# The opening of a two-branch kernel at the grain of one row: row 0 of 128 tokens ahead of row 1

## The chip, the cores and the metric

The kernel runs on one core of a Trainium2 chip. The metric is device time in microseconds (us) for one execution; the median of three runs of the kernel before is 198.41 us (198.15 to 198.58). Engines are named as in the profile: PE (matrix multiplication), PEld (its weight loads), DVE (vector engine), ACT (scalar engine, activation functions and copies), POOL, and SP, whose queue issues most loads.

## The reference, cut to what matters

```python
def reference(A_q, A_k, A_v, A_shift_k, A_ssm_k, A_ssm_D, B_x, B_w1, B_b1, B_w2, B_b2):
    ...
    x = A_q                                   # [1, 2048, 640] bf16
    xn = _layernorm(x, axis=-1)
    s = _A_ref(xn, A_k, A_v, A_shift_k, A_ssm_k, A_ssm_D)
    g = _silu(_B_ref(xn, B_w1, B_b1, B_w2, B_b2))
    return x + s * g
```

`_A_ref` multiplies a four-tap shifted k with v, convolves the product along the 2048 tokens with a 2048-long filter per channel (the reference does it by FFT), adds a D term and gates the result with xn. `_B_ref` is a feed-forward block, 640 to 1728 to 640, with a gelu between. Both branches read the normalised x, so the kernel opens with the normalisation.

## The kernel before, in words

The 2048 tokens lie as 16 tokens to each of 128 partitions. A "row" here is one token of each partition, a tile of 128 tokens by 640 channels; a "chunk" is four rows. The kernel computes the convolution as a two-stage transform by matmuls with sine and cosine matrices, and the feed-forward block chunk by chunk. After a function `prologue`, a hand-written order, `PLAN`, lists some 1,200 steps; each step issues its instructions, and each engine runs its own in that order. `PLAN` is not touched here. Each engine takes its instructions strictly in the order in which the program issues them for it, so an instruction that waits holds up all that stand behind it on the same engine.

`prologue` (L740 to L862) handles chunk 0 and prepares constants. What the change and the prediction's steps touch:

- `load_x` (L236) loads a chunk of x on SP's queue. Chunk 0 comes in two loads, rows 0 and 1, then rows 2 and 3. Behind them on the same queue stand three pieces of w1 (L266: columns 0 to 384, 384 to 768, the rest), then chunk 1, k and others.
- `build_f1_product` (L301) makes, after two index rows from POOL, a table of 16 x 128 products in one DVE instruction (L304). Its result is masked later (`f1_phase`, L308) and becomes the argument of sines on ACT at 28 us.
- `bn`, `ag` (L748, L751): statistics of half a row on DVE, two to a row, and their merge. `sq` (L754) takes the square root of variance plus epsilon on ACT, `rc` (L757) its reciprocal on DVE; both handle two rows at once. `norm_dve` (L760) normalises a row in place on DVE.
- `warm` (L766) issues matmuls of 512 columns whose result nobody reads; `WARM = (6, 7)` gives their numbers ahead of and behind the turning of the tap weights (L811).
- `turn` (L774) transposes one row into five 128 x 128 tiles on PE. Tiles 0 to 2 of two rows lie side by side in bank 6 of PSUM, tiles 3 and 4 in bank 7. `turned_out` (L780) copies one bank for both rows to xnT, bank 6 on DVE (L148) and bank 7 on ACT (L147).
- `first_block(x, i)` (L783) multiplies two rows (256 columns) with the i-th 128 columns of w1, five matmuls into bank i. Blocks 0 to 4 of rows 0 and 1 run ahead of the turning of rows 2 and 3, block 5 behind it, and then all six for rows 2 and 3.
- `tap` (L644) spreads tap weights over the partitions by four matmuls into banks 2 to 5; `tap_out` (L763) copies banks 2 and 3, then 4 and 5, to SBUF on ACT.
- `small_bits`, `small_first`, `small_second` (L347, L358, L365) are tiny DVE instructions that prepare the index tables of the small transform matrices. The first instruction of `small_second` is L356.
- An ACT instruction without a use (L848) brings the gelu table in ahead of the first gelu (L479). `pt` (L814) is the place in bank 7 where the biases are turned (L851), and L854 and L855 copy them out.

Behind `prologue`, DVE goes on with `s` (L377 to L385), `f1_phase` (L308), the statistics of chunk 1 (L421), its first products of k and the taps (L594), and the normalisation of rows 4 and 6 (L444), for which PE waits with the transposes of chunk 1 (L451).

Of the kernel before, what the change touches and what calls it, by code (L numbers as in the profile page):

```python
# [26 lines left out]
SIN_EPS = 2.0 ** -20  # L27

NSLOT = 48
WARM = (6, 7)  # L30
NFIRST = 6

TURNS = "231221331312001123202202330111320201303303312100"
# [58 lines left out]
def kernel(  # L92
# [15 lines left out]
    nc = tc.nc  # L108

    CH = 4  # L110
# [34 lines left out]
    def evac(eng, out_ap, in_ap):  # L145
        if eng == "a":
            return nc.scalar.copy(out=out_ap, in_=in_ap)  # L147
        return nc.vector.tensor_copy(out=out_ap, in_=in_ap)  # L148
# [3 lines left out]
    banks = psum.tile([P, 8, 512], F32, name="banks")  # L152
# [7 lines left out]
    ident = consts.tile([P, P], BF16, name="ident")  # L160
# [73 lines left out]
        return one(key).bitcast(BF16)  # L234

    def load_x(c):  # L236
        for h in range(1 if c else 2):
            js = slice(2 * h, CH if c else 2 * h + 2)
            nc.sync.dma_start(out=xn_tiles[c][:, js, :], in_=x_v[:, c * CH:(c + 1) * CH, :][:, js, :])

    def load_k(i):
# [56 lines left out]
    s16 = scratch([NJ], F32)  # L298
    r2 = scratch([P], F32)

    def build_f1_product():  # L301
        nc.gpsimd.iota(s16, pattern=[[1, NJ]], base=0, channel_multiplier=NJ, allow_small_or_imprecise_dtypes=True)
        nc.gpsimd.iota(r2, pattern=[[2, P]], base=1, channel_multiplier=0, allow_small_or_imprecise_dtypes=True)
        nc.vector.tensor_tensor(out=prod, in0=s16[:, :, None].to_broadcast([P, NJ, P]),  # L304
                                in1=r2[:, None, :].to_broadcast([P, NJ, P]), op=ALU.mult)
# [41 lines left out]
    def small_bits(*masks):  # L347
        for mask in masks:
            i = scratch([1], I32)
            nc.vector.tensor_single_scalar(out=i, in_=sm["kcol"], scalar=mask, op=ALU.bitwise_and)  # L350
# [7 lines left out]
    def small_first():  # L358
        n_in, c_in, r_in = sm["in"]
        n_out, c_out, r_out = sm["cols"]  # L360
        sm.update(ph=scratch([3, P], F32), mask=scratch([3, P], F32), c8=scratch([1], F32), c16=scratch([1], F32))
        nc.vector.tensor_single_scalar(out=sm["c8"], in_=c_in, scalar=8.0, op=ALU.mult)
        nc.vector.tensor_single_scalar(out=sm["c16"], in_=c_in, scalar=16.0, op=ALU.mult)
# [280 lines left out]
    def tap(j, h, ps):  # L644
        nc.tensor.matmul(out=ps[:, 0:HALF], lhsT=ident[0:4, j:j + 1].to_broadcast([4, P]), rhs=skT[:, half(h)],
                         start=True, stop=True)
# [93 lines left out]
    def prologue():  # L740
# [6 lines left out]
        def bn(j, h):  # L747
            nc.vector.bn_stats(out=stats[:, j, h, :], in_=xn[:, j, h * HALF:(h + 1) * HALF])  # L748

        def ag(j):  # L750
            nc.vector.bn_aggr(out=mv[:, j, :], in_=stats[:, j, :, :])  # L751

        def sq(a):
            nc.scalar.activation(out=sd[:, a:a + 2], in_=mv[:, a:a + 2, 1], func=ACT.Sqrt, bias=eps[:])  # L754

        def rc(a):
            nc.vector.reciprocal(out=rstd[:, a:a + 2], in_=sd[:, a:a + 2])  # L757

        def norm_dve(j):
            nc.vector.tensor_scalar(out=xn[:, j, :], in0=xn[:, j, :], scalar1=mv[:, j, 0:1],  # L760
                                    scalar2=rstd[:, j:j + 1], op0=ALU.subtract, op1=ALU.mult)

        def tap_out(j):  # L763
            nc.scalar.copy(out=halves(w_exp[:, j, :]), in_=banks[:, 2 * j + 2:2 * j + 4, 0:HALF])

        def warm(n, bank=7):  # L766
            for _ in range(n):
                nc.tensor.matmul(out=banks[:, bank, :].rearrange("p (a b) -> p a b", a=4), lhsT=ident[:],
                                 rhs=ident[:, None, :].to_broadcast([P, 4, P]), start=True, stop=True)

        split = (0, 3, DT)
        tp = [banks[:, 6 + b, :].bitcast(BF16).rearrange("p (t c) -> p t c", t=4) for b in range(2)]

        def turn(q):  # L774
            for t in range(DT):
                b = int(t >= split[1])
                nc.tensor.transpose(out=tp[b][:, t - split[b], q % 2 * P:(q % 2 + 1) * P],
                                    in_=xn[:, q, t * P:(t + 1) * P], identity=ident[:])

        def turned_out(eng, b, x):  # L780
            evac(eng, xnT[:, split[b]:split[b + 1], x * 2 * P:(x + 1) * 2 * P], tp[b][:, 0:split[b + 1] - split[b], :])

        def first_block(x, i):  # L783
            cols = slice(x * 2 * P, (x + 1) * 2 * P)
            for t in range(DT):
                nc.tensor.matmul(out=banks[:, i, cols], lhsT=w1_sb[:, t, i * P:(i + 1) * P], rhs=xnT[:, t, cols],
                                 start=(t == 0), stop=(t == DT - 1))
# [60 lines left out]
        nc.scalar.activation(out=sd[:, 0:1], in_=eps[:], func=ACT.Gelu_apprx_tanh)  # L848
        turn(2)
        turn(3)  # L850
        nc.tensor.transpose(out=pt[:, 0:FT + DT], in_=prm[:, :], identity=ident[0:FT + DT, 0:FT + DT])  # L851
        turned_out("d", 0, 1)
        turned_out("a", 1, 1)
        nc.vector.tensor_copy(out=b1_f[:], in_=pt[:, 0:FT])  # L854
# [56 lines left out]
```

## Time and profile before

| | |
|---|---|
| median of 3 runs | 198.41 us (198.15 to 198.58) |
| the profiled execution's own time | 198.26 us |
| its span in the profile | 196.5 us |
| granted clock of PE over the span | 0.998 |
| busy: PE, DVE, ACT, POOL | 186.5, 175.3, 162.6, 42.9 us |

A row of an engine's answer in order of time gives start, length, engine, line, operation, operands and how many instructions stand together; in brackets is the idle time ahead of the first and what ended it. Instructions of an engine overlap a little, so that several together take less than their single times. A row of busy time by stretch gives the stretch, its length, then the busy time of PE, PEld, DVE, ACT and POOL with the number of instructions, the granted PE clock, the share of DMA time and GB/s. A row of a group gives line, engine, operation, operands and shapes, the number, then busy us and mean ns of one, then the idle time ahead of them and its enders. A row of a load gives the median time from issue to landing at its end. In the chain of waits a row gives start, length and what ran.

### The profile page before, as it was taken

What the parts mean: (1) busy time and instruction counts of PE and PEld (TensorE: products, weight loads), DVE (VectorE), ACT (ScalarE), POOL (GpSimd) and SP (SyncE); (2) the same over time, 40 slices, a digit from 0 to 9 for tenths busy, and PEclk for the clock granted to TensorE, in tenths of its full rate; (3) what the DMA queues carried; (4) which work ended last, traced back from release to release, by engine and by line L of the source; (5) the groups of instructions that cost most, each with busy time, mean ns of one, the idle gap of its engine ahead of it and who ended that gap; (6) DMA issues with size and microseconds to landing.
All of it is one profiled execution on the core that took longest, in us unless ns stands there. A gap on an engine that the chain in (4) does not pass through costs nothing.

```text
span 196.5 us, 5128 instructions
## 1 busy us (share of the span) xinstructions
PE 186.5 (95%) x1927; PEld 111.1 (57%) x1939; DVE 175.3 (89%) x379; ACT 162.6 (83%) x323; POOL 42.9 (22%) x76
## 2 busy tenths in 40 slices
PE   7899969999999999998999999999999999999991
PEld 2585447787665445663566443465665544657771
DVE  7989999999999999989999999999999920489992
ACT  3577999999999999999998999999679758991030
POOL 8100300004454032344030000000475500002220
PEclk9999999999999999999999999999999999999999
DMA  6999999974888899798788999596969659994344
GB/s 200 374 378 345 342 408 414 393 294 153 319 326 337 268 325 368 303 341 341 267 274 312 287 338 329 158 303 228 272 243 336 223 188 350 397 398 157 145 173 137
DMA packets 27057, 57.69 MB, mean 294 GB/s; under 512 B 3032, under 2 KB 15513, under 8 KB 27032
## 3 DMA queue, kind: packets, MB, share of 16 engines
q1 hardware_dynamic: 22528, 39.65, 57.6%
q0 software_dynamic: 4320, 17.70, 24.3%
q8 instruction: 15, 0.25, 0.5%
q14 instruction: 10, 0.08, 0.2%
q10 hardware_dynamic: 184, 0.01, 0.1%
HBM read 33.76 MB, written 18.35 MB: 265 GB/s over the span
## 4 chain that ended last, share of the span: by engine, by line
PE 59%; ACT 14%; DMA 12%; DVE 9%; issue 3%; SPq 1%; DVEq 0%
PE banks L500 20%; PE banks L467 19%; ACT area L147 7%; PE banks L414 7%; DMA area<-in_A_k_dram 5%; DMA area<-in_A_ssm_k_dram 5%; PE banks L550 5%; DVE area L590 3%; DMA w_sb<-in_B_w_dram 2%; ACT hT L479 2%; DVE area L594 2%; PE banks L719 2%; PE banks L720 2%; DVE area L148 2%; PE banks L451 1%
## 5 line engine op out<-in xcount | busy, mean ns | idle before, releaser
L147 ACT CAST area<-banks 128x426 bf16<-128x426 f32 (+2 forms) x175 | 80.7, 614 | 4.2 <-PE banks L414 3.4
L500 PE MATMUL banks<-w_sb,hT 128*128 128x320 bf16 (+1 forms) x462 | 65.8, 295 | 0.4 <-ACT sl L508 0.3
L500 PEld LDWEIGHTS <-hT 128*128 128x128 bf16 x462 | 43.5, 98 | 18.9 <-issue 3.7
L467 PE MATMUL banks<-xnT,w_sb 128*128 128x512 bf16 x218 | 52.8, 379 | 0.7
L674 DVE TENSOR_TENSOR area<-banks,area 128x426 bf16<-128x426 f32 (+1 forms) x96 | 50.1, 591 | 0.2
L479 ACT ACTIVATE hT<-banks,b_f 128x512 bf16<-128x512 f32 x52 | 35.4, 718 | 4.9 <-PE banks L467 3.0
L467 PEld LDWEIGHTS <-w_sb 128*128 128x128 bf16 x230 | 21.5, 97 | 25.7 <-issue 3.7
L508 ACT ACTIVATE sl<-banks 128x320 bf16<-128x320 f32 (+1 forms) x33 | 14.8, 476 | 14.2 <-PE banks L500 12.9
L594 DVE TENSOR_TENSOR area<-area 128x1280 bf16<-128x1280 bf16 x32 | 25.4, 816 | 0.3
L414 PE MATMUL banks<-area,mats 32*32 32x426 bf16 (+1 forms) x768 | 20.7, 345 | 0.5 <-DVE area L148 0.2
L728 DVE TENSOR_TENSOR area<-banks,xn 128x426 bf16<-128x426 f32 (+1 forms) x18 | 9.9, 591 | 12.3 <-ACT hT L479 10.2
L704 POOL DMA_DIRECT2D scrC<-area x16 | 11.7, 730 | 42.1 <-ACT area L147 40.0
L590 DVE TENSOR_TENSOR area<-area 128x1280 bf16<-128x1280 bf16 x24 | 19.1, 812 | 0.0
L550 PE MATMUL banks<-area,WA 128*128 128x212 bf16 (+1 forms) x64 | 15.6, 299 | 0.1
L550 PE MATMUL banks<-area,WB 128*128 128x214 bf16 (+1 forms) x64 | 15.5, 299 | 0.0
L565 POOL DMA_DIRECT2D scrK<-area x16 | 8.8, 553 | 29.3 <-ACT area L147 28.9
L414 PEld LDWEIGHTS <-mats 32*32 32x32 bf16 x768 | 8.1, 88 | 12.4 <-issue 10.3
L148 DVE CAST area<-banks 128x426 bf16<-128x426 f32 (+1 forms) x21 | 11.4, 593 | 1.6 <-PE banks L414 0.8
L576 POOL DMA_DIRECT2D scrU<-area x16 | 8.6, 543 | 14.5 <-ACT area L147 13.7
L430 POOL TENSOR_TENSOR rs<-ve,mhalf 128x4 f32<-128x4 f32 x3 | 4.0, 1350 | 31.0 <-DVE ve L426 31.0
L421 DVE BATCH_NORM_STATS2 st<-xn 128x6 f32<-128x320 bf16 x24 | 10.3, 472 | 0.0
L515 DVE TENSOR_TENSOR xn<-xn,sl 128x320 bf16<-128x320 bf16 (+1 forms) x33 | 9.8, 307 | 0.2 <-ACT sl L508 0.2
(106 smaller groups left out, 195.8 us busy)
## 6 DMA issues: line engine op xcount, KB each, us to landing
scrK<-area POOLq DMA_DIRECT2D x16, 320.0 KB, 3.2
scrU<-area POOLq DMA_DIRECT2D x16, 320.0 KB, 3.7
area<-scrK SPq DMA_DIRECT2D x16, 320.0 KB, 6.6
area<-area SPq DMA_DIRECT2D x32, 160.0 KB, 3.8
area<-scrU SPq DMA_DIRECT2D x16, 320.0 KB, 4.8
scrC<-area POOLq DMA_DIRECT2D x16, 320.0 KB, 4.2
area<-scrC SPq DMA_DIRECT2D x16, 320.0 KB, 6.5
area<-in_A_k_dram SPq DMA_DIRECT2D x4, 640.0 KB, 10.0
```

Source lines behind the costliest of these rows:

```text
L147: return nc.scalar.copy(out=out_ap, in_=in_ap)
L148: return nc.vector.tensor_copy(out=out_ap, in_=in_ap)
L414: nc.tensor.matmul(out=out[b, :], lhsT=mats[a, m, a], rhs=rhs[a, :], start=start, stop=stop)
L467: nc.tensor.matmul(out=ps, lhsT=w1_sb[:, t, ft * P:(ft + 1) * P], rhs=xnT[:, t, :], start=(t == 0), stop=(t == DT - 1))
L479: nc.scalar.activation(out=hT[:, ft, :], in_=one(("h", i)), func=ACT.Gelu_apprx_tanh, bias=b1_f[:, ft:ft + 1], scale=1.0)
L500: nc.tensor.matmul(out=ps[:, 0:ws.stop - ws.start], lhsT=hT[0:M, ft, q * P:(q + 1) * P], rhs=w2_sb[0:M, ft, hs.start + ws.start:hs.start + ...
L508: nc.scalar.activation(out=sl[:, ws], in_=one(key)[:, 0:ws.stop - ws.start], func=ACT.Silu)
L550: nc.tensor.matmul(out=ps[:, dst], lhsT=(WA, WB)[r][:, n2, :], rhs=rows[:, n2 % 2, src], start=True, stop=True)
L590: nc.vector.tensor_tensor(out=uc, in0=uc, in1=tmp, op=ALU.add)
L594: nc.vector.tensor_tensor(out=tmp if s else uc, in0=kh[:, r0:r0 + KC, :], in1=w_exp[:, j:j + 1, :].to_broadcast([P, KC, D]), op=ALU.mult)
L674: nc.vector.tensor_tensor(out=flat(("p", i))[:, x * w:x * w + w], in0=one(("mu", i))[:, 0:w], in1=flat(key)[:, cols(j)], op=ALU.mult)
L704: nc.gpsimd.dma_start(out=pair_view(scrC)[g2], in_=pair(("c", g2)))
```

## The change

Chunk 0 is loaded as row 0 alone and rows 1 to 3 together. Square root and reciprocal are taken for row 0, for row 1, and for rows 2 and 3 together. A row's five transposed tiles now lie in one bank, bank 6 for even rows and bank 7 for odd ones; `turned_out` copies a range of tiles of one row: rows 0 and 1 in two pieces each on ACT, rows 2 and 3 in one piece each on DVE. `first_block` takes a range of rows: blocks 0 to 3 run for row 0 and for row 1 apart (128 columns), blocks 4 and 5 for both together. The product table is made in two instructions, 12 of its 16 parts at the old place and 4 behind the copies of rows 2 and 3, with `small_first` behind it. The warm-up matmuls are 6, 3 and 1 in place of 6 and 7. In DVE's order row 1's first statistics stand ahead of row 0's reciprocal, and row 2's first statistics ahead of row 1's. In ACT's order row 1's square root stands ahead of the copies of row 0, and the square root of rows 2 and 3 ahead of the second tap copy.

```diff
-WARM = (6, 7)
+WARM = (6, 3, 1)
...
     def load_x(c):
-        for h in range(1 if c else 2):
-            js = slice(2 * h, CH if c else 2 * h + 2)
+        for js in ((slice(0, CH),) if c else (slice(0, 1), slice(1, CH))):
             nc.sync.dma_start(out=xn_tiles[c][:, js, :], in_=x_v[:, c * CH:(c + 1) * CH, :][:, js, :])
...
-    def build_f1_product():
+    SPLIT = 12
+
+    def f1_indices():
...
+    def f1_product(a, b):
+        nc.vector.tensor_tensor(out=prod[:, a:b, :], in0=s16[:, a:b, None].to_broadcast([P, b - a, P]),
+                                in1=r2[:, None, :].to_broadcast([P, b - a, P]), op=ALU.mult)
...
-        def sq(a):
-            nc.scalar.activation(out=sd[:, a:a + 2], in_=mv[:, a:a + 2, 1], func=ACT.Sqrt, bias=eps[:])
+        def sq(a, n):
+            nc.scalar.activation(out=sd[:, a:a + n], in_=mv[:, a:a + n, 1], func=ACT.Sqrt, bias=eps[:])
...
-        tp = [banks[:, 6 + b, :].bitcast(BF16).rearrange("p (t c) -> p t c", t=4) for b in range(2)]
+        tp = [banks[:, 6 + b, :].bitcast(BF16)[:, 0:D].rearrange("p (t c) -> p t c", t=DT) for b in range(2)]
...
-        def turned_out(eng, b, x):
-            evac(eng, xnT[:, split[b]:split[b + 1], x * 2 * P:(x + 1) * 2 * P], tp[b][:, 0:split[b + 1] - split[b], :])
-
-        def first_block(x, i):
-            cols = slice(x * 2 * P, (x + 1) * 2 * P)
+        def turned_out(eng, q, a, b):
+            evac(eng, xnT[:, a:b, q * P:(q + 1) * P], tp[q % 2][:, a:b, :])
+
+        def first_block(i, lo, hi):
+            cols = slice(lo * P, hi * P)
...
-        build_f1_product()
+        f1_indices()
+        f1_product(0, SPLIT)
...
+        bn(0, 0)
+        bn(0, 1)
+        ag(0)
+        sq(0, 1)
         warm(WARM[0])
...
         warm(WARM[1])
-        pt = banks[:, 7, :].bitcast(BF16)[:, 4 * P:]
-        for j in (0, 1):
-            bn(j, 0)
-            bn(j, 1)
-            ag(j)
-        small_bits(30)
-        sq(0)
-        rc(0)
+        pt = banks[:, 7, :].bitcast(BF16)[:, D:]
+        bn(1, 0)
+        rc(0, 1)
         norm_dve(0)
-        norm_dve(1)
+        bn(1, 1)
+        ag(1)
+        sq(1, 1)
         turn(0)
-        turn(1)
...
+        warm(WARM[2])
         bn(2, 0)
-        turned_out("d", 0, 0)
-        turned_out("a", 1, 0)
+        turned_out("a", 0, 0, 3)
+        turned_out("a", 0, 3, DT)
         tap_out(0)
-        tap_out(1)
+        rc(1, 1)
+        norm_dve(1)
         bn(2, 1)
         ag(2)
         bn(3, 0)
+        first_block(0, 0, 1)
+        turn(1)
+        first_block(1, 0, 1)
+        turned_out("a", 1, 0, 3)
+        turned_out("a", 1, 3, DT)
         bn(3, 1)
         ag(3)
-        small_bits(1)
-        for i in range(NFIRST - 1):
-            first_block(0, i)
-        sq(2)
-        rc(2)
+        small_bits(30, 1)
+        sq(2, 2)
+        for i in (2, 3):
+            first_block(i, 0, 1)
+        tap_out(1)
+        for i in range(4):
+            first_block(i, 1, 2)
+        rc(2, 2)
         norm_dve(2)
         norm_dve(3)
         small_bits(96)
-        small_first()
-        nc.scalar.activation(out=sd[:, 0:1], in_=eps[:], func=ACT.Gelu_apprx_tanh)
+        first_block(4, 0, 2)
         turn(2)
         turn(3)
...
-        turned_out("d", 0, 1)
-        turned_out("a", 1, 1)
+        turned_out("d", 2, 0, DT)
+        turned_out("d", 3, 0, DT)
+        nc.scalar.activation(out=sd[:, 0:1], in_=eps[:], func=ACT.Gelu_apprx_tanh)
...
-        first_block(0, NFIRST - 1)
+        first_block(5, 0, 2)
+        f1_product(SPLIT, NJ)
+        small_first()
         small_second()
         for i in range(NFIRST):
-            first_block(1, i)
+            first_block(i, 2, CH)
```

More of the change, by code (lines that the diff above doesn't have):

```diff
@@ L751, in ag, with rc @@
             nc.vector.bn_aggr(out=mv[:, j, :], in_=stats[:, j, :, :])
-        def sq(a):
-            nc.scalar.activation(out=sd[:, a:a + 2], in_=mv[:, a:a + 2, 1], func=ACT.Sqrt, bias=eps[:])
-        def rc(a):
-            nc.vector.reciprocal(out=rstd[:, a:a + 2], in_=sd[:, a:a + 2])
+        def sq(a, n):
+            nc.scalar.activation(out=sd[:, a:a + n], in_=mv[:, a:a + n, 1], func=ACT.Sqrt, bias=eps[:])
+        def rc(a, n):
+            nc.vector.reciprocal(out=rstd[:, a:a + n], in_=sd[:, a:a + n])
         def norm_dve(j):
@@ L769, in warm @@
                                  rhs=ident[:, None, :].to_broadcast([P, 4, P]), start=True, stop=True)
-        split = (0, 3, DT)
-        tp = [banks[:, 6 + b, :].bitcast(BF16).rearrange("p (t c) -> p t c", t=4) for b in range(2)]
+        tp = [banks[:, 6 + b, :].bitcast(BF16)[:, 0:D].rearrange("p (t c) -> p t c", t=DT) for b in range(2)]
         def turn(q):
             for t in range(DT):
-                b = int(t >= split[1])
-                nc.tensor.transpose(out=tp[b][:, t - split[b], q % 2 * P:(q % 2 + 1) * P],
-                                    in_=xn[:, q, t * P:(t + 1) * P], identity=ident[:])
-        def turned_out(eng, b, x):
-            evac(eng, xnT[:, split[b]:split[b + 1], x * 2 * P:(x + 1) * 2 * P], tp[b][:, 0:split[b + 1] - split[b], :])
-        def first_block(x, i):
-            cols = slice(x * 2 * P, (x + 1) * 2 * P)
+                nc.tensor.transpose(out=tp[q % 2][:, t, :], in_=xn[:, q, t * P:(t + 1) * P], identity=ident[:])
+        def turned_out(eng, q, a, b):
+            evac(eng, xnT[:, a:b, q * P:(q + 1) * P], tp[q % 2][:, a:b, :])
+        def first_block(i, lo, hi):
+            cols = slice(lo * P, hi * P)
             for t in range(DT):
```

2 lines of the change are left out of this document (removed).

## The prediction

> **What bounds the kernel now.** I read the busy time by stretch first, then the order of time engine by engine over the first 27 us, then the waits.
>
> ```profile
> PE 186.5 (95%) x1927; PEld 111.1 (57%) x1939; DVE 175.3 (89%) x379; ACT 162.6 (83%) x323; POOL 42.9 (22%) x76
> ...
> 40.00:60.00 20.00, 19.87 (x153) 13.93 (x153) 19.93 (x37) 20.00 (x51) 8.27 (x15) 1.00 0.70 270
> ...
> 160.00:180.00 20.00, 19.82 (x129) 11.64 (x128) 9.45 (x18) 15.90 (x27) 0.58 (x2) 1.00 0.84 312
> ```
>
> From 40 us on, the matmul engine (first of the busy times behind the length) is busy for 99% of each stretch shown. Nothing after the opening is edited, so what the change is worth is how much sooner or later that full stretch begins. Its beginning is here:
>
> ```profile
> 26.52 1.31 PE L451 MATMUL banks<-ident,xn 128*128 128x128 bf16 x16 [1.45 <-DVE xn L444]
> ...
> 12.71 0.17 DVE L854 CAST b_f<-banks 128x14 f32<-128x14 bf16 x1 [0.29 <-ACT xnT L147]
> ...
> 12.87 0.60 DVE L356 SCALAR_TENSOR_TENSOR area<-area 128x128 f32<-128x128 f32 x2
> 16.56 0.88 DVE L421 BATCH_NORM_STATS2 st<-xn 128x6 f32<-128x320 bf16 x2
> 26.02 0.80 DVE L444 TENSOR_SCALAR xn<-xn,mv,rs 128x640 bf16<-128x640 bf16 x2
> ```
>
> The matmul engine runs dry at 25.07 and stands still for 1.45 us until DVE has normalised the second chunk (L444). DVE's answer shows no idle mark between 12.71 and 26.02, so DVE is a full line from L854 to L444. **The kernel's start-up is therefore DVE's line**, and the number to find is the moment at which DVE begins L356 (`small_second`), now 12.87. A lead of the matmul engine alone only lengthens its own 1.45 us of waiting.
>
> **What leads up to 12.87 now.**
>
> ```profile
> 1.64 2.29 DVE L304 TENSOR_TENSOR area<-area 128x2048 int32<-128x2048 f32 x1 [0.64 <-POOL area L303]
> 3.85 0.88 DVE L748 BATCH_NORM_STATS2 stats<-xn 128x6 f32<-128x320 bf16 x2
> 4.77 0.21 DVE L751 BATCH_NORM_AGGREGATE mv<-stats 128x2 f32<-128x12 f32 x1
> 4.89 0.83 DVE L748 BATCH_NORM_STATS2 stats<-xn 128x6 f32<-128x320 bf16 x2
> 6.39 0.17 DVE L757 RECIPROCAL rstd<-sd 128x2 f32<-128x2 f32 x1 [0.21 <-ACT sd L754]
> 6.60 0.80 DVE L760 TENSOR_SCALAR xn<-xn,mv,rstd 128x640 bf16<-128x640 bf16 x2
> ...
> 11.56 0.14 DVE L362 TENSOR_SCALAR area<-area 128x1 f32<-128x1 f32 x1
> 11.87 0.56 DVE L148 COPY xnT<-banks 128x768 bf16<-128x768 bf16 x1
> ...
> 1.35 2.74 PE L768 MATMUL banks<-ident 128*128 128x512 bf16 x6 [1.35 <-POOL ident masks.py:199]
> 4.65 1.69 PE L768 MATMUL banks<-ident 128*128 128x512 bf16 x7
> 7.10 0.81 PE L777 MATMUL banks<-ident,xn 128*128 128x128 bf16 x10 [0.77 <-DVE xn L760]
> 7.84 0.71 PE L645 MATMUL banks<-skT,ident 4*128 4x320 bf16 x4
> 8.48 2.90 PE L786 MATMUL banks<-xnT,w_sb 128*128 128x256 bf16 x25
> 11.22 0.72 PE L777 MATMUL banks<-ident,xn 128*128 128x128 bf16 x10
> 11.99 4.00 PE L786 MATMUL banks<-xnT,w_sb 128*128 128x256 bf16 x35
> ```
>
> Rows 2 and 3 are turned from 11.22, when the 25 matmuls of five blocks are through. Call that moment t. DVE's copy follows at 11.87, and L356 starts at t + 1.65.
>
> **The change part by part.** Prices: two statistics of a row and their merge, 4.77 - 3.85 = 0.92, with the next row 0.12 behind; the second of a pair starts some 0.40 after the first, as the two take 0.88 and overlap a little. The rest is priced by single instructions:
>
> ```profile
> L754 ACT ACTIVATE sd<-mv,eps 128x2 f32<-128x2 f32 x2 | 0.6, 295 | 1.0 <-DVE area L350 1.0
> L764 ACT CAST area<-banks 128x640 bf16<-128x640 f32 x2 | 1.3, 705 | 0.0
> L147 ACT COPY xnT<-banks 128x512 bf16<-128x512 bf16 x2 | 1.2, 585 | 1.8 <-PE banks L777 1.6 <-PE banks L851 0.2
> L147 ACT COPY area<-banks 128x640 bf16<-128x640 bf16 x5 | 3.2, 719 | 0.0
> L148 DVE COPY area<-banks 128x640 bf16<-128x640 bf16 x11 | 4.8, 483 | 0.0
> L760 DVE TENSOR_SCALAR xn<-xn,mv,rstd 128x640 bf16<-128x640 bf16 x4 | 1.6, 442 | 0.1
> L777 PE MATMUL banks<-ident,xn 128*128 128x128 bf16 x20 | 1.5, 220 | 0.8 <-DVE xn L760 0.8
> ```
>
> Two normalisations of 0.44 take 0.80, so DVE's instructions overlap by 0.08; two of ACT's casts (L764) of 0.70 take 1.3, so ACT's overlap by 0.1. A result is taken up on another engine about 0.05 later: normalised at 6.60 + 0.44 = 7.04, turned from 7.10.
>
> *Narrow matmuls.* Eight of the first blocks' halves become 128 columns wide: 40 matmuls in place of 20. No such matmul is in the trace. The nearest row is the transposes at 11.22, also 128 wide with a new weight each: (0.72 - 0.22)/9 = 0.056 apart. The wide ones stand (4.00 - 2.90)/10 = 0.110 apart, so by this row the split costs 40 x 0.056 - 20 x 0.110 = 0.04 us, next to nothing. The other end is the transposes of L451, 16 in 1.31 with a wait inside, (1.31 - 0.22)/15 = 0.073. I take 0.056, since those ran with all operands there.
>
> *The loads.* Row 0 comes alone, rows 1 to 3 behind it; SP issues two loads as before, so all that queues behind them on SP (w1, the next chunk, K) keeps its place.
>
> ```profile
> xn<-in_A_q_dram SPq DMA_DIRECT2D x2, 320.0 KB, 3.5
> skp<-in_A_shift_k_dram ACTq DMA_DIRECT2D x1, 5.0 KB, 3.2
> ...
> 0.73 0.39 SPq L239
> ...
> 1.18 0.42 SPq L239
> ...
> 1.64 4.56 DMA w_sb<-in_B_w_dram
> ```
>
> The second load lands at 1.18 + 3.5 = 4.68; the bytes up to there are the same, so rows 1 to 3 should land then too. The first was in by 3.85, when DVE read it without waiting. For row 0 alone the ends are 3.36 (DVE is free of three quarters of L304, 1.64 + 0.75 x 2.29) and 3.93 (0.73 and the 3.2 of the 5 KB load: a small load is hardly quicker). I take 3.5. DMA: Bandwidth & Descriptors, section "Anatomy of one DMA", in the Trainium skill says, of loads that POOL issues, that one costs a fixed 2 us and its bytes at 436 GB/s, so halving it saves little; by its figures 160 KB less saves an estimated 0.38 us, 3.85 - 0.38 = 3.47, and the sum stays as it is. The 5 KB row agrees that the fixed part rules.
>
> *DVE and ACT up to t.* Row 0's statistics start at about 3.5 and are merged at 3.5 + 0.92 + 0.21 = 4.63, its square root is there at 4.97. The next instruction in DVE's order is row 1's statistics, which **wait for rows 1 to 3 until 4.70**; the reciprocal and normalisation of row 0 queue behind them. So: reciprocal 5.10 (0.40 behind row 1's first half), normalisation 5.31 to 5.75 (6.60 - 6.39 = 0.21 behind), turned from 5.81, done 6.25. Any landing of row 0 up to 3.6 gives the same. Row 1: second half 5.67, merge 6.19 to 6.40, square root on ACT 6.44, reciprocal 6.76, normalised 6.97 to 7.41. ACT copies row 0 after that square root: 384 and 256 wide, 0.45 and 0.32 by the slope between 585 ns at 512 and 719 at 640, done 7.32. Block 0 of row 0 ends at 7.56 (now: two rows from 8.48), row 1 is turned at 7.6, blocks 1 to 3 of row 0 run from 8.0 to 8.84, row 1's four blocks to 9.96 (20 x 0.056). The first piece of w1 lands at 1.64 + 4.56 = 6.20, so it holds nothing up. Block 4 writes a bank that the second tap copy (L764) must have left: DVE's statistics of rows 2 and 3, begun behind row 1's merge, go round row 1's normalisation (7.33, 7.97, 8.37) to a last merge ended 9.10; square root 9.14, tap copy 9.34 to 10.04, block 4 from 10.1, five wide matmuls. **t = 10.65**, 0.57 earlier than 11.22. Two chains, matmuls and statistics, arrive within 0.14 of each other.
>
> *DVE after t.* Now DVE copies one half and ACT the other. Then DVE copies both rows: first at t + 0.49 (five transposes, 4 x 0.056 + 0.22, and 0.04 of signalling), the second 0.40 later, and b1 at t + 1.29. DVE itself, behind four bit operations, the reciprocal, two normalisations (9.7 to 10.43) and two more bit operations, is ready at 10.75, so the copy waits 0.4 us: an idle gap, into which nothing has been put. The last quarter of L304, 0.57 and some 0.04 fixed, now stands on the line, with L362 and its twin, 0.13, and the two small copies before them, 0.16. L356 starts at t + 2.19 = 12.84, against 12.87 now. **The shift is -0.03 us**; it becomes a loss when t comes after 10.68.
>
> *Hidden.* Warm-up matmuls, 13 to 10: they ran beside DVE's statistics. ACT's added work, one square root (0.30) and 1.54 of copies for 1.17, falls into its idle time ahead of 7.95 and still leaves the gelu table ready near 11.5; if that cover were gone, the first gelu would be late by up to the 1.28 us of the table load.
>
> ```profile
> 10.37 1.28 ACT L848 ACT_TABLE_LOAD   x1
> 13.29 1.84 ACT L479 ACTIVATE hT<-banks,b_f 128x512 bf16<-128x512 f32 x3 [0.61 <-PE banks L786]
> ```
>
> The matmul engine ends the opening some 0.5 us earlier; that goes into the gap at 25.07.
>
> Against the profiled execution's 198.26 us the sum gives 198.23; that execution lies 0.15 below the median of the three runs, 198.41, so the same shift on the median gives 198.38. I predict **198.3**.
>
> **Rivals.**
> *The matmul lead comes through (faster).* If the trace's wait at 26.52 hides a matmul bound, the 0.5 us of lead reach the end: 197.8. For it: PE is fullest over the whole span. Against: the 1.45 us. 20%.
> *Row 2 is turned late (slower).* Place: PE from 8.0 to t. At 0.073 the 35 narrow matmuls there take 0.6 more, less 0.14 of slack: t = 11.1, L356 at 13.3, 198.7. It decides from t = 10.68 on. For it: L451; against: 11.22's own row. 20%.
> *Row 0 is not ahead (the change does not do what it says).* Landing at 3.93 starts its statistics at 3.98, and its reciprocal, 1.49 later, at 5.47 in place of 5.10: t = 11.0, 198.6. For it: the 5 KB load. 10%.
> *The clock falls.* The first six warm matmuls take 2.74 us, the seven at 4.65 only 1.69, so the engine starts at half speed. TensorE: Matmul & The Clock Gate, in the Trainium skill, Parts 1 and 4, says that a window of 3.4 us without activity halves the clock and that transposes do not count as activity. With fewer warm matmuls, a fall at 8.0 would double the 2.5 us of matmul work between 8.0 and t, 2.3 more behind the slack of 0.14: 200.5. Against:
>
> ```profile
> 4.60:8.00 3.40, 2.63 (x21) 1.28 (x20) 3.01 (x12) 1.03 (x3) 1.26 (x1) 1.00 1.09 354
> 192.40:195.70 3.30, 0.00 (x0) 0.00 (x0) 0.63 (x3) 0.30 (x1) 0.00 (x0) 1.00 0.38 125
> 195.80:196.50 0.70, 0.00 (x0) 0.00 (x0) 0.00 (x0) 0.00 (x0) 0.00 (x0) 0.50 0.00 0
> ```
>
> The clock stays at 1.00 through 3.3 us without any matmul at the end and is 0.50 only after; the changed opening leaves no gap over 0.6 us. 5%.
>
> **How the numbers follow.** The forecast has 45%, with its own range 198.0 to 198.5: rows 1 to 3 landing early enough not to be waited for gives 0.21 us less, t two tenths late gives as much more. 0.2%, 0.4 us, is about what a measurement of this kernel can tell. Faster by more: the first rival and 5 of the forecast's 45, 25%. Slower: the late turn, the clock, half of row 0's case and 4 of the forecast's, 34%. Within: 41%. The range 197.7 to 199.0 takes in the lead at one end and, at the other, the late turn together with a late row 0; it leaves the clock out.
>
> **What would show it.** Row 0's normalisation near 5.3, not 6.6; a wait of DVE on a load at 4.7; first blocks from about 7.2; narrow matmuls 0.056 apart; rows 2 and 3 turned at 10.65; an idle mark on DVE's copy there; L356 of now at about 12.85; and the gap at 25.07 grown to about 2 us with its end unmoved. The forecast is wrong if that gap's end moves by over 0.4 us, or if the end moves without it.

## The result, and the profile after

The changed kernel takes **198.72 us** (median of 20 runs, 198.31 to 202.69) against 198.39 us (20 runs, 198.15 to 199.36) of the kernel before beside it. The ratio is 1.0021, 95% interval 1.0012 to 1.0031: slower by about 0.2%. That ratio leaves out the most disturbed runs; the counts by granted clock below are over all runs. The profiled execution takes 198.46 us with a span of 196.7, against 198.26 and 196.5.

The opening in the changed kernel's profile, in order of time (start, length, engine, line, operation, operands, count, and in brackets the idle time ahead and what ended it):

```profile
1.65 1.76 DVE L307 TENSOR_TENSOR area<-area 128x1536 int32<-128x1536 f32 x1 [0.64 <-POOL area L304]
3.32 0.88 DVE L751 BATCH_NORM_STATS2 stats<-xn 128x6 f32<-128x320 bf16 x2
...
4.66 1.38 PE L771 MATMUL banks<-ident 128*128 128x512 bf16 x3
...
5.18 0.49 DVE L751 BATCH_NORM_STATS2 stats<-xn 128x6 f32<-128x320 bf16 x1 [0.73 <-DMA xn<-in_A_q_dram]
...
5.77 0.45 DVE L763 TENSOR_SCALAR xn<-xn,mv,rstd 128x640 bf16<-128x640 bf16 x1
...
6.28 0.45 PE L778 MATMUL banks<-ident,xn 128*128 128x128 bf16 x5 [0.24 <-DVE xn L763]
...
7.42 0.45 DVE L763 TENSOR_SCALAR xn<-xn,mv,rstd 128x640 bf16<-128x640 bf16 x1
...
8.27 2.90 PE L786 MATMUL banks<-xnT,w_sb 128*128 128x128 bf16 x40
...
9.54 0.29 ACT L757 ACTIVATE sd<-mv,eps 128x2 f32<-128x2 f32 x1 [0.32 <-DVE area L353]
9.74 0.67 ACT L767 CAST area<-banks 128x640 bf16<-128x640 f32 x1
...
11.01 0.72 PE L778 MATMUL banks<-ident,xn 128*128 128x128 bf16 x10
...
11.49 0.89 DVE L148 COPY xnT<-banks 128x640 bf16<-128x640 bf16 x2 [0.36 <-PE banks L778]
...
12.45 0.68 DVE L307 TENSOR_TENSOR area<-area 128x512 int32<-128x512 f32 x1
...
13.17 0.61 DVE L359 SCALAR_TENSOR_TENSOR area<-area 128x128 f32<-128x128 f32 x2
...
26.32 0.80 DVE L447 TENSOR_SCALAR xn<-xn,mv,rs 128x640 bf16<-128x640 bf16 x2
...
26.82 1.31 PE L454 MATMUL banks<-ident,xn 128*128 128x128 bf16 x16 [1.87 <-DVE xn L447]
```

And of its loads, the one of rows 1 to 3 (KB, and us from issue to landing):

```profile
xn<-in_A_q_dram SPq DMA_DIRECT2D x1, 480.0 KB, 4.0
```

Row 0 is ahead: it was there by 3.32, when DVE came free, and it is normalised at 5.77, where before both rows waited until 6.60. But DVE stands idle for 0.73 us before 5.18: **rows 1 to 3 come half a microsecond later than the second load did before**, 4.0 us behind their issue where the second load took 3.5. All that follows row 1's statistics is held up by it. Row 1 is normalised at 7.42, the last statistics reach ACT's square root at 9.54, the tap copy behind it ends at 10.41, block 4 waits for that copy, and rows 2 and 3 are turned at 11.01. Then the copies and the last quarter of the product table (12.45) bring the first instruction of `small_second`, now L359, to 13.17, against 12.87: **0.30 late**. The gap of the matmul engine ends at 26.82, not 26.52: 0.30 again. Set side by side in order of time, the instructions of PE and DVE are 0.30 late from 27 us on, those of ACT from some 40 us on, and all are 0.36 late at the end. The matmul engine's lead, 0.12 us between 13 and 24 us, gains nothing: it and the 0.30 of lateness lengthen the idle time ahead of L454 from 1.45 to 1.87 (below, "the gap").

That is one loss. The second does not show in this profile, but in the single runs. Each run comes with its mean granted clock: 12 of the 20 lie at 0.997 or above, with a median of 198.51, and 8 lie at 0.986 to 0.992, six of them at 198.95 to 199.35, the others at 200.13 and 202.69. One stretch of 3.41 us at half clock takes 0.5 x 3.41/196.7 = 0.009 off the mean: the clock falls about once in these eight. Of the kernel before, 2 of 113 runs in four later comparisons had such a mean.

### The profile page after: what moved, and what is told of

Same layout as the page of the kernel before. It is cut to its first block, busy times and chain, and to the rows that moved or that the text cites. A ratio compares the mean times of both kernels' runs of the same rounds, so it can differ in the third digit from the quotient of the medians.

```text
span 196.7 us, 5179 instructions
## 1 busy us (share of the span) xinstructions
PE 187.6 (95%) x1956; PEld 111.2 (57%) x1956; DVE 175.3 (89%) x381; ACT 163.3 (83%) x326; POOL 43.0 (22%) x76
## 4 chain that ended last, share of the span: by engine, by line
PE 64%; ACT 14%; DMA 12%; DVE 5%; issue 2%; SPq 1%; ACTq 0%; DVEq 0%
PE banks L503 23%; PE banks L470 19%; ACT area L147 8%; PE banks L417 7%; DMA area<-in_A_k_dram 6%; PE banks L553 5%; DMA area<-in_A_ssm_k_dram 5%; PE banks L542 2%; ACT hT L482 2%; DMA xn<-in_A_q_dram 2%; PE banks L722 2%; PE banks L454 2%; PE banks L723 2%; DVE area L593 2%; DVE area L148 2%
## 5 line engine op out<-in xcount | busy, mean ns | idle before, releaser
L470 PE MATMUL banks<-xnT,w_sb 128*128 128x512 bf16 x230 | 53.6, 379 | 0.1
```

Source lines behind the costliest of these rows:

```text
L470: nc.tensor.matmul(out=ps, lhsT=w1_sb[:, t, ft * P:(ft + 1) * P], rhs=xnT[:, t, :], start=(t == 0), stop=(t == DT - 1))
```

## The experiments

Three questions: what makes L359 late; where the clock falls, and why; and whether a version without both losses beats the kernel before. "Fell" counts runs with a mean granted clock under 0.993; "held" is the median of the others. "Before beside it" is the median of the kernel before in the same comparison. A held run can be long for another reason: for example, five of e12's lie at 201 and more, two of e10's near 200.

| kernel | L359 or L356 in its profile | median (runs) | before beside it | held | fell |
|---|---|---|---|---|---|
| changed | 13.17 | 198.72 (20) | 198.39 | 198.51 | 8 |
| e1 rows 0-1 | 13.06 | 198.50 (12) | 198.29 | 198.43 | 3 |
| e6 three loads | 13.16 | 199.14 (12) | 198.31 | 198.57 | 5 |
| e7 seven warm | 13.00 | 199.01 (12) | 198.31 | 198.65 | 5 |
| e10 fill | 14.58 (fell) | 198.49 (12) | 198.16 | 198.40 | 2 |
| e2 whole table | 14.89 (fell) | 197.95 (12) | 198.29 | 197.94 | 1 |
| e11 whole, fill | 12.58 | 197.96 (12) | 198.16 | 197.87 | 3 |
| e8 whole, seven warm, rows 0-1 | 12.51 | 198.19 (12) | 198.31 | 198.19 | 0 |
| e13 whole, seven warm, fill | 12.65 | 197.95 (12) | 198.26 | 197.95 | 0 |
| e5 before, row 0 alone | 13.24 | 198.56 (12) | 198.29 | 198.56 | 0 |
| e4 before, three warm | 13.07 | 199.88 (12) | 198.29 | 198.66 | 8 |
| e12 before, three warm, fill | 12.88 | 201.08 (12) | 198.16 | 201.15 | 5 |
| e9 before, quarter moved | 13.63 (fell) | 199.60 (9) | 198.31 | 198.80 | 6 |

### The loads

**e5**: the kernel before, with the loads of the changed one.

```diff
-            js = slice(2 * h, CH if c else 2 * h + 2)
+            js = slice(h, CH if c or h else 1)
```

> The kernel before with the loads of the change alone: row 0, then rows 1 to 3. Theory of the late landing: row 1's statistics wait until about 5.2 in place of 4.89, all of DVE's work up to the turning moves by 0.3, and the time becomes 198.7. Rival, that rows 1 to 3 landed late in the changed kernel by chance of one execution: 198.4.

In its profile, in order of time:

```profile
5.21 0.89 DVE L748 BATCH_NORM_STATS2 stats<-xn 128x6 f32<-128x320 bf16 x2 [0.23 <-DMA xn<-in_A_q_dram]
...
13.24 0.61 DVE L356 SCALAR_TENSOR_TENSOR area<-area 128x128 f32<-128x128 f32 x2
...
26.89 1.31 PE L451 MATMUL banks<-ident,xn 128*128 128x128 bf16 x16 [1.46 <-DVE xn L444]
```

Row 1's statistics start at 5.21, so the late landing (5.18 in the changed kernel) comes from the cut of the loads alone. L356 is 0.37 late, the gap's end 0.37, and every engine 0.38 at the end. The medians differ by 0.27, and the ratio is 1.0008 (0.9994 to 1.0021): the delay is plain in the trace, but in the time not clear of noise.

It is not the chance of one execution either. From issue to landing the second load takes 3.8 to 4.1 us in nine of the ten profiles with row 0 alone, 5.1 in e2's, and 3.5 to 3.8 in the six with rows 0 and 1 together. In the changed kernel's profiles with an undisturbed opening (the first, and e15 and e16 below), row 1's statistics start at 4.98, 5.18 and 5.32, and L359 follows at 12.99, 13.17 and 13.30. Why the same bytes land later in this cut, no run shows.

**e1**: the changed kernel with the loads of before, rows 0-1 and rows 2-3.

```diff
-        for js in ((slice(0, CH),) if c else (slice(0, 1), slice(1, CH))):
+        for js in ((slice(0, CH),) if c else (slice(0, 2), slice(2, CH))):
```

> The changed kernel with the loads of before: rows 0 and 1 together, then rows 2 and 3; all else as changed. Theory of the DVE line: row 1's statistics no longer wait for a load (they waited until 5.18), DVE's first statistics start at about 3.85 in place of 3.32, row 0's normalisation at about 5.55 in place of 5.77, the small phases (13.17 in the changed kernel, 12.87 before) at about 12.95, and a run whose clock holds takes 198.46 - 0.2 = 198.25. Rival, that PE's narrow matmuls or ACT's copies set the late turning of row 2: the phases stay at 13.1 to 13.2 and the time at 198.45.

```profile
3.91 0.89 DVE L751 BATCH_NORM_STATS2 stats<-xn 128x6 f32<-128x320 bf16 x2 [0.50 <-DMA xn<-in_A_q_dram]
4.95 0.44 DVE L751 BATCH_NORM_STATS2 stats<-xn 128x6 f32<-128x320 bf16 x1
...
10.90 0.72 PE L778 MATMUL banks<-ident,xn 128*128 128x128 bf16 x10
...
13.06 0.60 DVE L359 SCALAR_TENSOR_TENSOR area<-area 128x128 f32<-128x128 f32 x2
```

Row 1 no longer waits, but row 0 comes 0.5 after DVE is free, so t is 10.90 and L359 13.06, 0.11 later than expected: without the early row 0 the gain is half (and no more than the 0.18 by which the changed kernel's own L359 moves, 12.99 in e15), and the moved quarter of the product table still costs more than the earlier turning returns.

**e6**: three loads, so that row 1 does not come with rows 2 and 3.

```diff
+        for js in ((slice(0, CH),) if c else (slice(0, 1), slice(1, 2), slice(2, CH))):
```

> The changed kernel with chunk 0 in three loads: row 0, row 1, rows 2 and 3. Theory of the late landing: the wait of row 1's statistics for a load (until 5.18 in the changed kernel) is gone, row 0's normalisation starts near 5.0 in place of 5.77, the small phases near 12.5 to 12.7 in place of 13.17, and a run whose clock holds takes 198.0 in place of 198.5. Rival, that the one more issue on SP (0.4 us) makes the first piece of w1 late and PE waits for it: the phases stay at 13.1 and the time at 198.5.

```profile
4.36 0.44 DVE L751 BATCH_NORM_STATS2 stats<-xn 128x6 f32<-128x320 bf16 x1
...
9.06 2.11 PE L786 MATMUL banks<-xnT,w_sb 128*128 128x128 bf16 x30 [0.21 <-DMA w_sb<-in_B_w_dram]
...
13.16 0.61 DVE L359 SCALAR_TENSOR_TENSOR area<-area 128x128 f32<-128x128 f32 x2
```

Row 1's wait is gone (4.36), but w1 stands one issue further back and the first blocks now wait for it: L359 is where it was. The theory fails here, and the rival named with it is what happened.

### The product table

**e2**: the whole table at the old place, ahead of the landing.

```diff
-        f1_product(0, SPLIT)
+        f1_product(0, NJ)
...
-        f1_product(SPLIT, NJ)
```

> The changed kernel with the product table made whole at the old place, before the first statistics, nothing behind the copies of rows 2 and 3. Theory of the DVE line: the first statistics start at 3.85 in place of 3.32, still ahead of the load that row 1's wait for (5.18), so nothing ahead of the turning moves; the 0.59 us of the last quarter leaves DVE's line, the small phases start at about 12.6, and a run whose clock holds takes 198.46 - 0.59 = 197.9. Rival, that PE or ACT and not DVE sets the end of the opening: 198.3 to 198.5.

**e9**: the kernel before with only the last quarter moved.

```diff
+        f1_product(0, 12)
...
+        f1_product(12, NJ)
         small_second()
```

> The kernel before with the last quarter of the product table moved behind the copies of the biases, as in the change, all else as before. Theory of the DVE line: 0.6 us more on a line without a gap; the small phases start at 13.4 to 13.5 in place of 12.87, PE's gap before the second chunk's transposes ends 0.5 to 0.6 later, the time is 198.3 + 0.55 = 198.85. Rival, that PE's line is the bound: 198.3 to 198.4.

Held runs of e2 have a median of 197.94, 0.57 under the changed kernel's: the quarter's 0.68 us (the row at 12.45) come through to the end almost whole, as DVE's line being the bound demands. (e2's profiled run itself was one with a late landing and a fallen clock, below.) Held runs of e9 lie at 198.8, 0.5 above before, with the sign turned; its L359 is at 13.63, 0.76 behind the L356 of before: 0.60 for the quarter, and 0.16 because rows 0 and 1 came later in this run, so that the first statistics start at 4.01 and not at 3.85.

### Where the clock falls

e9's profiled run shows a fall. Its stretches of 3.41 us, each with its length, the busy time of PE, PEld, DVE, ACT and POOL, the granted clock, the DMA share and GB/s:

```profile
21.29:24.70 3.41, 3.41 (x18) 1.53 (x16) 3.41 (x8) 2.97 (x7) 1.48 (x1) 1.00 1.09 341
24.70:28.12 3.42, 1.29 (x14) 0.62 (x13) 3.31 (x6) 3.40 (x5) 0.00 (x0) 1.00 1.03 406
28.12:31.53 3.41, 3.41 (x20) 2.21 (x18) 3.41 (x7) 3.40 (x5) 0.00 (x0) 0.50 1.03 412
31.53:34.94 3.41, 3.41 (x29) 2.48 (x28) 3.38 (x7) 3.38 (x2) 0.00 (x0) 1.00 1.03 412
```

The matmul gap of 2.06 us before L454 lies wholly in the stretch 24.70 to 28.12, in which PE is busy for 1.29 us; the next stretch runs at half clock. In all profiles the clock changes on such a **grid of 3.41 us**, whose place against the program's start differs from run to run. The records of the granted clock show it: in e9 they begin at 4.22 and the fall comes at 28.12, 23.90 us or 7 stretches later; in e16 (below) it is 4.47 and 28.36, again 7, in e14 14.22 and 31.28, 5 stretches; in the changed kernel's first profile the clock holds from 5.82 to 196.96, 56 stretches. TensorE: Matmul & The Clock Gate in the Trainium skill, Part 1, says so too (a free-running window of 3413 ns). The same page of the Trainium skill, in "Why this matters for your kernels", asks for matmul gaps under about 3 us; here 2.06 was long enough for a fall.

Is this what happens to the changed kernel? Its own profile held, so it was run three times more for its profile alone.

> The changed kernel once more, for its profile alone: 8 of its 20 runs had a mean granted clock of 0.986 to 0.992, and the profile taken of it held. Two places are possible. Theory (the second chunk): where the clock falls, the records show 0.50 for one stretch of 3.41 us that begins between 25 and 30 us, with L359 still near 13.2 and a time of 198.9 to 199.4. Rival (the opening): 0.50 begins between 7 and 9 us, L359 comes near 14.6 and the time is 199.7 to 200.2. A profile that holds says nothing on this.

> The same kernel a second time, with the same two expectations: 0.50 from 25 to 30 us and 198.9 to 199.4 by the theory, 0.50 from 7 to 9 us and 199.7 to 200.2 by the rival.

> The same kernel a third time, with the same two expectations: 0.50 from 25 to 30 us and 198.9 to 199.4 by the theory, 0.50 from 7 to 9 us and 199.7 to 200.2 by the rival.

e15 held: 198.21, L359 at 12.99. e14 took 202.38 and e16 199.34, and both show the fall in the second chunk, right behind the gap at 25 us (in e14 later than expected, at 31.28, because its whole opening was some 3 us late, see the end). Of e16, two rows in order of time, then its stretches:

```profile
13.30 0.60 DVE L359 SCALAR_TENSOR_TENSOR area<-area 128x128 f32<-128x128 f32 x2
...
26.96 1.31 PE L454 MATMUL banks<-ident,xn 128*128 128x128 bf16 x16 [1.87 <-DVE xn L447]
```

```profile
24.95:28.36 3.41, 1.47 (x19) 1.11 (x19) 3.38 (x6) 3.38 (x5) 0.00 (x0) 1.00 1.03 408
28.36:31.77 3.41, 3.41 (x16) 2.00 (x14) 3.41 (x7) 3.41 (x4) 0.00 (x0) 0.50 1.02 411
```

And e14's:

```profile
27.87:31.28 3.41, 1.47 (x18) 0.88 (x17) 3.30 (x7) 3.39 (x5) 0.00 (x0) 1.00 1.04 416
31.28:34.70 3.42, 3.42 (x17) 2.01 (x15) 3.42 (x6) 3.41 (x5) 0.00 (x0) 0.50 1.01 407
```

In both the gap of 1.87 us lies wholly in one stretch, 1.47 us of PE work are left in it, and the next stretch is at half clock. Against the changed kernel's first profile, e16 is 0.14 late up to the gap and 0.78 late behind the fall: the fall costs 0.64 us. (Right behind the fall, up to 36 us, PE is 1.80 late, 1.66 more than at the gap, about the half of 3.41 that the slow stretch loses; by 45 us all but 0.64 of it is made up.) Where the gap is cut by a grid point, the clock holds, as in the first profile of the changed kernel and in those of e1, e7 and e15. The changed kernel's first profile, then e6's with the gap just whole, then that of before:

```profile
22.88:26.30 3.42, 2.07 (x10) 0.75 (x8) 3.31 (x6) 3.23 (x6) 0.48 (x1) 1.00 1.06 401
26.30:29.71 3.41, 2.82 (x29) 2.18 (x30) 3.41 (x7) 3.38 (x5) 0.00 (x0) 1.00 1.02 406
29.71:33.12 3.41, 3.41 (x30) 2.50 (x28) 3.41 (x8) 3.38 (x4) 0.00 (x0) 1.00 1.04 420
```

```profile
23.64:27.05 3.41, 1.53 (x9) 0.51 (x6) 3.30 (x8) 3.20 (x6) 0.00 (x0) 1.00 1.05 389
27.05:30.47 3.42, 3.35 (x36) 2.69 (x36) 3.42 (x7) 3.41 (x4) 0.00 (x0) 1.00 1.03 412
```

```profile
25.09:28.51 3.42, 1.92 (x23) 1.52 (x24) 3.42 (x7) 3.39 (x6) 0.00 (x0) 1.00 1.02 407
28.51:31.92 3.41, 3.41 (x29) 2.53 (x28) 3.41 (x8) 3.41 (x3) 0.00 (x0) 1.00 1.03 417
```

So at this place the clock fell behind 1.47 us busy and held behind 1.53. A whole gap of 1.87 in one stretch is thus not enough: in e14 and e16 a pause of 0.07 us between the transposes behind the gap lies in the same stretch, in e6 it lies behind the grid point. Before, the whole gap of 1.45 lies in the stretch, 1.92 us are still busy, and the clock held. From the gap's start to that pause's end it is 2.23 us (24.95 to 27.18 in the changed kernel's first profile), so the chance that one stretch takes in both is, as an estimate, (3.41 - 2.23)/3.41 = 0.35. Of the runs of the four kernels with that gap (changed, e1, e6, e7) and the three repeats, 23 of 59 fell, 0.39. Some of these fell in the opening, which costs more (next): leaving out those above 199.8, but for e14, 17 of 59 are left, 0.29.

**e10** fills the gap: six matmuls of 512 columns, read by nobody, ahead of the first transposes, in their bank.

```diff
         tp = one_bf(("tt", i))
+        if not filled:
+            filled.append(i)
+            for _ in range(FILL):
+                nc.tensor.matmul(out=one(("tt", i)).rearrange("p (a b) -> p a b", a=4), lhsT=ident[:],
+                                 rhs=ident[:, None, :].to_broadcast([P, 4, P]), start=True, stop=True)
```

> The changed kernel with six 512-wide dummy matmuls of the identity ahead of the first transposes of chunk 1, in the transposes' own bank: they fill some 1.4 us of matmul idle time that was 1.87 us long before 26.82 and change nothing on VectorE's line. Theory (the clock falls because of that gap): the transposes still start near 26.8 in a profile that lands like the changed kernel's, and the mean granted clock is 0.995 or more in nearly all runs (0 or 1 of 12 below, against 8 of 20), so the median becomes the changed kernel's undisturbed 198.5 with no run over 199. Rival (the clock falls in the opening, ahead of 12 us): 4 or 5 of 12 runs still fall to 0.986 to 0.992 and take 199 to 200. Third way (the fill itself delays the transposes, because their bank comes free late): gap's end later by 0.3 or more, median 198.8 with no falls.

Falls drop from 8 of 20 to 2 of 12, which alone could be chance. But neither costs what a fall in the second chunk costs, 0.4 to 0.8 us in the six runs above: no run lies between 198.75 and 199.69. So at that price there is none in 12, against up to 17 in 59. The time did not follow: e10's median is still 0.33 above the kernel before beside it, with a ratio of 1.0025 (1.0003 to 1.0047). The profiled run is one of the two:

```profile
4.38:7.80 3.42, 2.38 (x18) 1.01 (x16) 2.43 (x9) 1.63 (x5) 1.49 (x1) 1.00 1.08 355
7.80:11.21 3.41, 3.41 (x35) 3.41 (x33) 3.19 (x15) 2.96 (x7) 0.00 (x0) 0.50 1.06 418
...
24.86:28.28 3.42, 2.85 (x14) 1.13 (x13) 3.31 (x7) 3.23 (x5) 0.00 (x0) 1.00 1.03 411
```

It fell **in the opening**, at 7.80, which costs more: rows 2 and 3 are turned at 12.43 instead of 11.01 and the run takes 199.84, 1.44 above the held median. e2's fall was of this kind:

```profile
4.72:8.13 3.41, 1.47 (x11) 0.67 (x12) 1.95 (x8) 0.94 (x3) 1.14 (x1) 1.00 1.07 347
8.13:11.54 3.41, 3.41 (x27) 2.62 (x26) 2.94 (x13) 2.56 (x8) 0.00 (x0) 0.50 1.06 418
```

Two runs of e10, 199.92 and 200.01, had a held clock; what delayed them is not known.

### The warm-up matmuls

**e4**, before with `WARM = (6, 3)`; **e7**, changed with `WARM = (6, 7, 1)`; **e12**, e4 with the fill of e10.

> The kernel before with 3 warm-up matmuls in place of 7 behind the tap weights. Theory of the clock: the long runs of the changed kernel, whose mean clock is 0.986 to 0.991, come from fewer warm-up matmuls; then about a third of the runs here show such a clock too and take 199 or more, the rest 198.4. Rival, that the grain of one row itself brings the clock down: no run here has a clock below 0.995, all take 198.2 to 198.6.

> The changed kernel with 7 warm-up matmuls in place of 3 behind the tap weights (6, 7, 1). Theory of the clock: nearly no run has a mean clock under 0.993 (8 of 20 in the changed kernel), and the median is that of the changed kernel's runs with a held clock, 198.5. Rival, that the clock falls for the grain of one row itself: a third of the runs stay under 0.993, the median 198.7.

> The kernel before with 3 instead of 7 warm matmuls, which fell in 8 of 12 runs (199.8 to 200.2), and with the same fill ahead of chunk 1's transposes. If its falls sit in the opening (matmul idle 0.97 us ahead of 7.30, with little behind it), they stay: 6 or more of 12 near 199.9, and a profile that falls shows 0.50 between 7 and 12 us. If they sit behind the gap at 25 us (1.46 us there), they go: median 198.4.

e4's falls (8 of 12, all at 199.8 to 200.2) cost about 1.5 us, like those seen in the opening; its gap at 25 us is 1.46, as in the kernel before, whose clock held there. The fill does not take them away: in e12 5 of 12 fell, one fewer than expected, three at 199.84 to 199.91 and two at 201.4 and 201.6; five more runs at 201.0 to 201.5 had a held clock. So in the kernel before, the seven warm-up matmuls are what keeps the clock up: with three, 8 of 12 fell, with seven 1 of 35 beside them. That these falls lie in the opening is read from their price and from e12, since no profile of a fallen run of e4 or e12 was taken. In the changed kernel, adding the warm-up matmuls (e7) left 5 falls of 12, against the theory that their lack causes the falls. The gap was still there, in e7's profile:

```profile
26.65 1.31 PE L454 MATMUL banks<-ident,xn 128*128 128x128 bf16 x16 [1.87 <-DVE xn L447]
```

### Versions without these losses

**e8** is the changed kernel with e2's whole table, seven warm-up matmuls and e1's loads; **e11** is e2 with e10's fill; **e13** is e11 with seven warm-up matmuls.

> The changed kernel with three of its parts put back: rows 0 and 1 in one load, the product table made whole ahead of the statistics, 7 warm-up matmuls. What stays is the turning, the copies and the first blocks row by row. If the prices add: the phases start 0.11 + 0.59 ahead of the changed kernel's 13.17, at 12.5, no clock under 0.993, the time 198.5 - 0.1 - 0.59 = 197.8, faster than the kernel before by 0.25%. Rival, that the statistics, then 0.53 later, come to set the turning: no better than 198.2.

> The changed kernel with the whole product table ahead of the loads' landing and with the same fill. Theory (VectorE's line sets the end, the gap sets the falls): 197.9 like the undisturbed runs of the kernel with the whole table, faster than before by 0.4, and no falls at 25 us; a rare late landing of rows 1 to 3 can still cause one in the opening (1 of 12). Rival (the fill takes matmul time that the end feels): 198.3 or more.

> The changed kernel with the whole product table ahead of the landing, 7 warm matmuls as before and the six dummy matmuls ahead of chunk 1's transposes: both stretches in which the matmul engine idles are shortened. Theory: 197.9 in undisturbed runs, at most 1 of 12 with a fallen clock, median 197.9 to 198.0, faster than before by 0.3. Rival (the warm matmuls delay row 0's turning, or the opening's falls come from late loads and not from too few warm matmuls): falls in 3 or more of 12, with 199.2 to 199.8.

In e8, whose profile gives

```profile
12.51 0.60 DVE L359 SCALAR_TENSOR_TENSOR area<-area 128x128 f32<-128x128 f32 x2
...
26.16 1.31 PE L454 MATMUL banks<-ident,xn 128*128 128x128 bf16 x16 [1.27 <-DVE xn L447]
```

L359 is 0.36 earlier than before, the gap ends 0.36 earlier and is down to 1.27 us, and no run fell. The end is only 0.28 earlier in the profile, and the median 0.12 under before, less than expected. With the whole table the gap at 25 us is 1.27 (e2's too), and no fall there was seen even without the fill. e11 and e13 differ in the warm-up matmuls alone: with three, 3 of 12 fell, with runs of 199.15 to 199.75; with seven, none; numbers this small can be chance. e13's profiled L359 is at 12.65, 0.22 early, and its end 0.21 early. Its median is 197.95 against 198.26, ratio 0.9982, interval 0.9955 to 1.0008. e8 has 0.9987 (0.9973 to 1.0001), e2 0.9988 (0.9967 to 1.0009), and e11, with its falls, 1.0005 (0.9982 to 1.0029). None is clear of 1: by the medians a gain of some 0.1 to 0.3 us is likely, not shown.

## Why the prediction was wrong

The forecast was no change, 198.3; it came out slower by 0.3 us and 0.2%. Two steps failed, the landing of the second load and the price of a longer gap.

- **The first step that failed** is that of the loads: "the bytes up to there are the same, so rows 1 to 3 should land then too", at 4.68. They were there at 5.18 (4.98 to 5.32 in the three repeats and e7, 6.33 in e2's profiled run), 4.0 us and not 3.5 behind their issue. That the bytes up to there are the same did not fix the landing. e5 shows that the cut of the loads does it without the rest of the change. What follows was sized right: t = 11.01 for 10.65, with the square root at 9.54 for 9.14; L359 at t + 2.16 for t + 2.19. The sentence "it becomes a loss when t comes after 10.68" thus held. Two rivals named times near this, t = 11.1 and 198.7 for the late turning, t = 11.0 and 198.6 for a late row 0. That was luck, since neither narrow matmuls nor row 0 were late.
- **Narrow matmuls**: right. The 35 narrow ones and block 4's five take 2.90 us, and until block 4 waits for the tap copy they run 0.056 apart.
- **Row 0's landing**: by 3.32, below all bounds (3.65 in e14's profile), but without use, because its reciprocal still queues behind row 1's late statistics: normalised at 5.77 for 5.31.
- **The idle mark at the copy**: 0.36 for 0.4, right. The moved quarter cost what it was priced at (e11, which leaves it in place, has L359 0.59 earlier), and the idle 0.36 was not used for it.
- **DVE's line as the bound**: right. Shifts of L359 between -0.36 and +0.37 came through to the gap's end one to one in e5, e8 and the changed kernel, and to the ends of their profiles within 0.08. The rival that the matmul lead reaches the end is refuted: the lead of 0.12 ended in the gap.
- **"That goes into the gap at 25.07"** was right as a place and wrong as a price of nothing. The gap grew to 1.87, not 2, and behind a gap of that length the clock falls in some runs: e14 and e16 show it, and e10, which fills most of the gap, shows no such fall. Costing a lead at nothing because it ends in idle time was the second failed step. By the prediction's own sum the gap would have grown to about 2 and the falls would have come just the same; its sign, an end of the gap moved by over 0.4 us, would not have told, as that end moved by 0.30.
- **The clock rival** had the mechanism, with 5% and at 8.0, 200.5. Its ground against, that the clock held through 3.3 us without a matmul, was misread. It comes from the program's end: the last matmul ends at 192.36, the grid of that profile (first record at 4.61) has points at 192.35 and 195.76, and the clock falls at 195.76. One stretch idle, the next at 0.50, is what happens behind the gap too. Falls at its place exist (e10 and e2, 199.84 and 200.08), but the changed kernel's two recorded ones, and by their price six of its eight, are behind the gap at 25 us. TensorE: Matmul & The Clock Gate in the Trainium skill, Part 1, speaks of an idle window; here the clock fell behind stretches in which PE was busy for 1.29 to 1.47 us of 3.41.

Of the 0.33 us between the medians, 198.51 - 198.39 = 0.12 is left among the runs whose clock held; by this the rest comes from the falls. The profiled executions differ by more, 0.20, because that of before lies 0.13 under its median and that of the changed kernel 0.05 under the held one. But the split is not firm: in e10, without the falls behind the gap, the held runs are 0.25 above the kernel before beside it, and all its runs 0.33. Both steps are shown by traces and edits; how much of the 0.33 each of them costs stays open.

## What to carry to other kernels

Cutting one load so that its first piece comes early moved the rest of the same bytes later here: ask who waits for the last piece. When an engine gains time ahead of a wait that stays, its idle time grows there, and here a longer gap of the matmul engine had a price of its own, because it let the clock fall; count the falls over many runs, since one profile can miss them. Dummy matmuls in the gap took these falls away and cost little that could be seen between e2 and e11 (held runs 0.35 and 0.29 under the kernel before beside them); that they also made the changed kernel faster is not shown.

## What the runs showed of the hardware that was not expected

- The clock is set by stretches of 3.41 us on a grid that lies differently from run to run, so one program has two times (e15 held, e16 fell). Behind the gap at 25 us a stretch with 1.47 us of PE work lowered the next one, one with 1.53 did not. In the opening 2.38 us lowered it (e10), and 2.41 did not (e16's stretch from 4.47): there part of the work is transposes and matmuls over four rows. Busy time alone is thus not the measure; what is stays open.
- The release at the start can come very late. e14's records of the granted clock begin at 14.22 us, not at 4.2 to 6.6 as elsewhere; until then it ran at about half pace: the narrow matmuls stand 0.107 apart, not 0.056, the 40 of the first blocks take 4.84 us for 2.90, and the run took 202.38:

```profile
9.68 4.84 PE L786 MATMUL banks<-xnT,w_sb 128*128 128x128 bf16 x40
```

The changed kernel's run of 202.69, e2's of 201.30, e4's of 201.62 and e12's at 201 and more may be of this kind, but no profile of them was taken.
